# Kernel spectra from the compressed kernel in one dense matmul step; input spectra and tap sums in smaller TensorE tiles; a new task order

## The chip, the cores and the metric

The kernel runs on one core of a Trainium2 chip. The core has five engines that run their own instruction queues and wait for each other through semaphores: TensorE (PE, matmuls; its weight loads are listed apart as PEld), VectorE (DVE), ScalarE (ACT), GpSimd (POOL) and SyncE (SP, which issues transfers). Matmuls write to PSUM; DVE and ACT carry the results from there to SBUF (an "eviction"). Transfers between device memory and SBUF run on 16 DMA engines and are issued from the SP, POOL or ACT queue. The metric is the time of one execution on the device in microseconds (us); a profile is one execution recorded by the hardware profiler.

## What is computed

Two branches over the same input x (2048 positions, 640 channels, bf16), mixed by a gate. Branch A is attention with 32 heads of 20 channels in which each position sees eight positions at distances 0, 2, ... 14. Branch B is a state-space convolution: per channel a kernel K of length 2048, a real part of a sum over 192 complex exponentials, is convolved with the channel through a Fourier transform of length 4096.

```python
g = sigmoid((x * gate_w).sum(-1, keepdims=True))
# A
logits = einsum("bhsd,bhswd->bhsw", q, kg) * scale        # w: 8 taps, dilation 2
o = einsum("bhsw,bhswd->bhsd", softmax(logits), vg);  a = o @ wo
# B
l = arange(L).astype(bfloat16)                            # positions rounded to bf16
P = exp(logdA[:, :, None] * l)
K = einsum("dn,dnl,dn->dl", Cc, P, dB).real
y = irfft(rfft(u, 2 * L) * rfft(K, 2 * L))[:L] + u * Dskip
return g * a + (1 - g) * y
```

Since the positions are rounded to bf16, K takes few distinct values at large l: for each channel 32 x 20 values (times 8 i + m with i below 32 and m from a list of 20, `MS`, plus one more m, 2048, for the last four positions, 21 in all) hold the whole kernel. This is the "compressed kernel", tile E.

## The kernel before

Every piece of work is a task with an engine, an estimated duration and dependencies. Two plans exist, "main" and "tail"; in each the order of the tasks is a list written into the source (`ORDER`, L52), which also says on which engine ("A" for ACT, "D" for DVE) an eviction runs. `Plan.emit` (L150) issues them in that order, and each engine and each transfer queue works strictly in order.

Main plan. (1) SSM parameters (`SSMParams`, DVE and ACT, the first 40 us). (2) The input is turned and projected to q, k, v (`plan_late`, matmul L311, PSUM tile "tb"); v goes to device memory (vS). (3) The kernel generator (`KGen.plan`): ten chunks of 16 channels a group, each with 15 argument matmuls (L801, PSUM "ar"), 15 sine or exponential activations on ACT (L816, L818) into a ring of buffers, products on DVE (L838, L840: "pt", "qq") and 256 small matmuls (L856, PSUM "kps"), evicted to E. After five chunks a half of the channels ("hf") is complete. (4) Attention (`plan_core`) in eight tiles of 256 positions: for each the shifted v is fetched (`loadv`, "vc", L368, POOL queue), products on DVE ("prod", L375), logits on PE (L381), a softmax, the weights written to memory and fetched spread over the partitions ("asb", L428), products with v on DVE ("pv", L449), the sum over the taps on PE (`gather`, L456), and the output projection (L480) whose result is scaled by the gate ("ga", L489) and stored (gaS). Before, the partitions of "vc" are 64 rows of heads and halves times two groups of taps, each group holding four taps in its free dimension, and `gather` runs as 128x64 tiles of the PE array, two of them side by side.

(5) Kernel expansion (`KExpand`, L875): for each half, E is shifted between partitions by two small matmul groups (L895), copied out on DVE into the full kernel in time order (X, 11 copies, L903), written to memory (Kx, L929 to L932) and read back transposed (kc, L938). (6) First Fourier step (`first`, L1300, and `split`, L1319): matmuls of 256 columns with the constants F1k for the kernel and F1c for the input (Usb), evicted 1024 elements a partition to bufA (kernel) and big (input). The input's first step has to wait for the last generator product, since the ring lies in big.

Tail plan (`fft_conv`, L1024). For each of eight frequency blocks, the second Fourier step: four spectra (kernel and input, real and imaginary part) in two halves each, four matmuls of 320 columns per half (L1073, PSUM "fp") with a basis PHI, evicted as "sp_k" and "sp_u"; then six products and sums on DVE ("ta", "tc" L1101, "Y" L1104). Then the inverse transform in two steps (L1134, evictions "bufA<-cp"; L1164) and the mix with the gate, the attention result (gaF) and the store (L1170 to L1191). Transfers for the tail's constants (psi) and gaF are paced by the blocks (L1087).

Of the kernel before, what the change touches and what calls it, by code (L numbers as in the profile page):

```python
# [11 lines left out]
ALU = mybir.AluOpType  # L12
# [8 lines left out]
S = 2048  # L21
D = 640
# [5 lines left out]
VW = 256 + 3 * DIL  # L28
# [10 lines left out]
def _attn_consts():  # L39
    ind = np.zeros((128, 96), np.float32)  # L40
    for h in range(32):
        ind[4 * h:4 * h + 4, h] = 1.0
    for r in range(64):
        ind[[r, 64 + r], 32 + r] = 1.0
# [49 lines left out]
), "tail": (  # L94
# [21 lines left out]
class Plan:  # L116
# [21 lines left out]
    def order(self):  # L138
        out, at = [], 0
        for x in ORDER[self.name].split():  # L140
            at += int(x.rstrip("ADSG"))
            t = self.tasks[at]
            t.eng = x[-1] if x[-1] in "ADSG" else next(iter(t.dur))
            out.append(t)
        for n, t in enumerate(out):
            t.place = n
        assert len(out) == len(self.tasks) and all(d.place < t.place for t in out for d in t.deps + t.after)
        return out
# [20 lines left out]
class Attn:  # L169
# [80 lines left out]
    def consts(self, cst):  # L250
        nc = self.nc
        ind_np, ident_np, mask0_np = _attn_consts()
        self.ind = cst.tile([128, 96], BF16, name="ind")
# [7 lines left out]
    def load_wo(self, _):  # L261
        wv = self.wo.rearrange("(r a e) c -> a r e c", a=2, e=5)
        for a in range(2):
            self.nc.gpsimd.dma_start(self.wo_sb[64 * a:64 * a + 64], wv[a])
# [1134 lines left out]
```

## Time and profile before

| | |
|---|---|
| time, median of three runs | 337.42 us (335.88 to 338.04) |
| span of the profiled execution | 335.4 us |
| busy: PE, weight loads | 285.5 us (85%), 171.0 us (51%) |
| busy: DVE, ACT, POOL | 294.2 us (88%), 293.4 us (87%), 62.3 us (19%) |
| transfers | 45.68 MB, mean 136 GB/s |
| granted TensorE clock, mean | 0.98 of full speed |

The span runs from the first to the last instruction; the time of a run also holds what lies around it. "Busy" for PE counts pipelined matmuls from start to modelled end, so that a busy PE is not one at its peak. In the views below a row of the groups reads: line, engine, operation, tile written <- tiles read, shapes, number of instructions | busy us together, mean ns of one | idle time of the engine just before them and what ended it. A row of the timeline begins with the start and the length in us. A row of the windows gives, for a stretch of time, the busy us (and the instructions) of PE, weight loads, DVE, ACT and POOL, the granted clock, the share of the DMA engines and GB/s.

### The profile page before, as it was taken

The page shows a single profiled execution, that of the slowest core. Times are in us where ns is not written, and L with a number is a line of the kernel's source. Part 1 is how long each engine was busy: PE and PEld are TensorE (multiplying, and loading weights), DVE is VectorE, ACT ScalarE, POOL GpSimd, SP SyncE. Part 2 cuts the span into 40 slices and gives each one's busy share as a digit, 9 for nine tenths or more (in the row PEclk, how much of TensorE's full clock was granted, in tenths as well). Part 3 has the DMA queues.
Part 4 walks back from the last instruction along what each step waited for, and adds up shares of the span by engine and source line. Part 5 has one row for each costly group of instructions (what it writes and reads, how often), then busy time and mean ns, then how long its engine had stood idle before and what let it go on. Part 6 is the DMA issues. An engine that isn't in the chain of part 4 may idle for free. (4 is left out here: it accounts for less than half of the span.)

```text
span 335.4 us, 11982 instructions
## 1 busy us (share of the span) xinstructions
PE 285.5 (85%) x5181; PEld 171.0 (51%) x5214; DVE 294.2 (88%) x401; ACT 293.4 (87%) x433; POOL 62.3 (19%) x94
## 2 busy tenths in 40 slices
PE   0367999997899999999998799999999899996850
PEld 0334563444445555445554344556677676665740
DVE  1997988798989999999999979999686799999881
ACT  1789736999899999999999799999987889998990
POOL 8700043020005000101412341211040000000062
PEclk9999999999999999999999989999999999999985
DMA  8984435437107110524874887365565527666056
GB/s 253 356 264 113 119 91 159 86 91 170 26 9 153 27 24 8 149 62 141 199 190 119 186 208 161 93 118 124 154 207 221 180 64 216 159 123 100 4 136 182
DMA packets 45975, 45.68 MB, mean 136 GB/s; under 512 B 25098, under 2 KB 39738, under 8 KB 45922
## 3 DMA queue, kind: packets, MB, share of 16 engines
q1 hardware_dynamic: 39928, 27.90, 30.3%
q0 software_dynamic: 5248, 16.39, 20.2%
q8 instruction: 41, 0.67, 0.9%
q10 hardware_dynamic: 746, 0.61, 0.6%
q14 instruction: 12, 0.10, 0.1%
HBM read 30.88 MB, written 14.01 MB: 134 GB/s over the span
## 5 line engine op out<-in xcount | busy, mean ns | idle before, releaser
L311 PE MATMUL tb<-bufA 128*128 128x512 bf16 x267 | 73.5, 391 | 4.2 <-issue 1.4
L816 ACT ACTIVATE big<-ar 128x740 bf16<-128x740 int16 (+1 forms) x72 | 56.7, 858 | 1.4 <-PE ar L801 1.2
L818 ACT ACTIVATE big<-ar 128x848 bf16<-128x848 f32 x60 | 50.1, 905 | 0.2
L801 PE MATMUL ar<-Rarg,L 64*128 64x212 bf16 (+4 forms) x600 | 46.5, 253 | 3.5 <-ACT big L816 1.9
L449 DVE TENSOR_TENSOR pv<-vc,asb 128x2048 bf16<-128x2048 bf16 x40 | 48.2, 1217 | 0.3 <-PE tb L456 0.3
L311 PEld LDWEIGHTS <-bufA 128*128 128x128 bf16 x300 | 31.2, 122 | 28.5 <-issue 12.3
L856 PEld LDWEIGHTS <-pt 128*32 128x32 bf16 (+1 forms) x2560 | 25.3, 92 | 35.7 <-issue 33.2
L856 PE MATMUL kps<-qq,pt 128*32 128x21 bf16 (+1 forms) x2560 | 36.6, 173 | 6.0 <-issue 5.1
L838 DVE TENSOR_TENSOR pt<-big 128x1024 bf16<-128x1024 bf16 x48 | 32.8, 701 | 4.3 <-ACT big L816 2.2
L801 PEld LDWEIGHTS <-L 64*128 64x128 bf16 x600 | 20.8, 94 | 25.2 <-issue 22.4
L480 PE MATMUL tb<-wo_sb,oT 128*128 128x320 bf16 x160 | 29.9, 306 | 0.2
L507 ACT ACTIVATE sp_u<-fp 128x640 bf16<-128x640 f32 x31 | 23.9, 953 | 0.8 <-PE fp L1073 0.8
L375 DVE TENSOR_TENSOR prod<-prj 128x2048 bf16<-128x2048 bf16 x20 | 24.0, 1218 | 0.2 <-PE lg L381 0.2
L375 DVE TENSOR_TENSOR prod<-qA,kA 128x2048 bf16<-128x2048 bf16 x20 | 23.9, 1217 | 0.2 <-PE lg L381 0.2
L507 ACT ACTIVATE sp_k<-fp 128x640 bf16<-128x640 f32 x29 | 22.6, 969 | 1.1 <-PE fp L1073 1.1
L456 PE MATMUL tb<-pv,ind 128*64 128x512 bf16 (+1 forms) x192 | 23.2, 353 | 0.0
L368 POOL DMA_DIRECT2D vc<-vS x16 | 11.5, 723 | 59.0 <-DVE pv L449 55.0
L840 DVE TENSOR_TENSOR qq<-big 128x1344 bf16<-128x1344 bf16 x24 | 21.2, 883 | 0.0
L1191 POOL DMA_DIRECT2D out_dram<-ot x14 | 7.7, 558 | 72.3 <-DVE ot L1173 72.3
L1073 PEld LDWEIGHTS <-PHI 128*128 128x128 bf16 x160 | 15.5, 97 | 8.1 <-issue 1.1
L489 ACT ACTIVATE ga<-tb,g_sb 128x320 bf16<-128x320 f32 x29 | 15.6, 550 | 3.4 <-PE tb L480 3.1
L480 PEld LDWEIGHTS <-oT 128*128 128x128 bf16 x160 | 13.1, 98 | 7.1 <-issue 3.1
(171 smaller groups left out, 547.9 us busy)
## 6 DMA issues: line engine op xcount, KB each, us to landing
vc<-vS POOLq DMA_DIRECT2D x16, 327.5 KB, 6.4
xn<-in_A_x_dram SPq DMA_DIRECT2D x4, 640.0 KB
gaS<-ga SPq DMA_DIRECT2D x8, 320.0 KB
Usb<-in_A_x_dram POOLq DMA_DIRECT2D x8, 320.0 KB, 5.7
gaF<-gaS SPq DMA_DIRECT2D x8, 320.0 KB
bufA<-in_A_wqkv_dram SPq DMA_DIRECT2D x3, 800.0 KB
Sprm<-pc SPq DMA_DIRECT2D x10, 240.0 KB
L<-Sprm SPq DMA_DIRECT2D x76, 30.0 KB
```

The lines of the kernel that those rows point to most:

```text
L311: nc.tensor.matmul(ppf, self.wq[:, which, kt, e::5], self.xT[:, c0 // 1024, kt, c0 % 1024:c0 % 1024 + SC], start=(kt == 0), stop=(kt == NK ...
L375: nc.vector.tensor_tensor(b[e][:], q[:, e, o:o + C].unsqueeze(1).to_broadcast([128, W, C]), win(k[:, e, :], o, W, DIL, C), ALU.mult)
L449: nc.vector.tensor_tensor(o, vw, b["asb"][:].unsqueeze(2).to_broadcast(sh), ALU.mult)
L456: nc.tensor.matmul(b["op", e][64 * a:64 * a + 64, 0:n, :], ind[:, 32:96], b["pv", e][:, w, a, 0:n, :], start=(w == 0), stop=(w == 3), skip ...
L480: nc.tensor.matmul(apf[:, :320], b["oT"][:, e, i * 128:(i + 1) * 128], wo_sb[:, e, hf * 320:(hf + 1) * 320], start=(e == 0), stop=(e == 4))
L507: nc.scalar.activation(o, i, ACT.Identity)
L801: nc.tensor.matmul(ar[:, g2, a0:a0 + ncol], L[rows, sb, gv, l0:l0 + 128], R[rows, c0:c0 + ncol], start=True, stop=True, tile_position=(64 ...
L816: nc.scalar.activation(d_[:, :, s0 * QW:s1 * QW], ar[:].bitcast(I16)[:, :, 0:2 * (s1 - s0) * QW:2], ACT.Sin, scale=SCL)
L818: nc.scalar.activation(dst[:, gp::2].rearrange("p g s n -> p g (s n)"), ar[:, :, 0:2 * EW], ACT.Exp)
L838: nc.vector.tensor_tensor(pt[:, :, k, :], gg[:, :, ::-1] if k else gg, e1, ALU.mult)
L840: nc.vector.tensor_tensor(qq[:], trg[:, :, KI:].rearrange("p a (v m) -> p a v m", v=2), exq[:, :, KI:].unsqueeze(2).to_broadcast([128, 32, ...
L856: nc.tensor.matmul(kps[32 * g:32 * g + 32, h, NM * ql:NM * ql + NM], pt[rows, k, v, :], qq[rows, k, v, :], start=(g not in started), stop= ...
```

## The change

1. The expansion of the kernel and its first Fourier step are dropped. A constant "km" of 128 x 20,480 values (eight blocks of 640 KB) maps the 640 compressed values of a channel directly to its 2048 frequencies: contraction over 128 partitions (32 i times four m) and five steps k. The class KSpread stores E of a half to memory with four transfers and reads it back with m on the partitions (tile T); `dense` does 20 matmuls of 160 columns for two of a block's four f. They run on 128x64 tiles of the array, two side by side, with km as the weights and T as the moving data.
2. Half 0's kernel spectra for all eight blocks are made in the main plan (`spectra`, 16 evictions of 640 elements), half 1's in the tail, block by block ("kd", 16 evictions). The blocks of the tail run in the order 5, 6, 7, 0, ... 4, since the last three km tiles of the main plan stay in their three slots.
3. The input's Fourier steps use 64x64 tiles of the array: `first` does 16 matmuls of 128 columns where it did four of 256, and the second step ("up") 16 matmuls of 160 columns for a half spectrum where it did four of 320.
4. Attention's shifted v is laid out as 32 heads times four groups of two taps: four copies a tile of 256 positions (32 rows, all groups) instead of two; "asb" is one transfer of half the bytes; `gather` runs on 128x32 tiles, four side by side, with half the columns per PE pass, and in smaller tasks; wo is laid out to match (four loads).
5. The term of the kernel's last four positions (m = 2048) is no longer in the kernel spectrum: POOL works out running sums of the first input rows times that value (`lag`), and eight small matmul pairs ("sel") add it in the last step.
6. A new order of all tasks, with other choices between ACT and DVE: E evictions 10 and 0 become 7 and 3, "ga" 29 and 3 become 22 and 10, v evictions 7 and 3 become 4 and 6.

```diff
-class KExpand:
...
+class KSpread:
...
+    def store(self, hf, E):
+        for mm in range(4):
+            self.nc.sync.dma_start(self.Ed[hf, mm].rearrange("g i c k -> (g i) c k"), E[:, :, 5 * mm:5 * mm + 5].rearrange("p c m x -> p c (m x)"))
+    def load(self, hf):
+        for mm in range(4):
+            self.nc.sync.dma_start(self.T[hf][32 * mm:32 * mm + 32].rearrange("i g c k x -> i g (c k x)"), self.Ed[hf, mm].rearrange("g i c k -> i g (c k)"))
+def dense(nc, o, km, T, ro, fs):
+    for f in fs:
+        for k in range(5):
+            for h in range(2):
+                rhs = bass.AP(T.tensor, T[:, 0, 0, k, 20 * h].offset, [list(T.ap[0]), [400, 4], [220 - 40 * h, 2], [1, 20]])
+                nc.tensor.matmul(o[64 * h:64 * h + 64, f, 0:160].rearrange("p (g j x) -> p g j x", j=2, g=4), km[:, k, ro, f, :], rhs,
+                                 start=(k == 0), stop=(k == 4), skip_group_check=True, tile_position=(0, 64 * h))
+def dense_out(nc, en, dst, o):
+    evict(nc, en, dst.rearrange("p j (x g) f -> p (j x) g f", g=4), o[:, :, 0:160].rearrange("p f (g x) -> p x g f", g=4))
...
+    def load_km(n, fb):
+        o = KM0 + KMW * (n % 3)
+        nc.sync.dma_start(P["bufA"][:, o:o + KMW], km_d[:, fb])
...
-                b["vc"] = aq.tile([128, 2, 5, VW], BF16, name="vc")
-                for w2 in range(2):
-                    nc.gpsimd.dma_start(b["vc"][64 * w2:64 * w2 + 64]...)
+                b["vc"] = aq.tile([128, 4, 5, VW], BF16, name="vc")
+                for w4 in range(4):
+                    nc.gpsimd.dma_start(b["vc"][32 * w4:32 * w4 + 32]...)
...
+                    for t in range(2):
+                        for a in range(4):
+                            nc.tensor.matmul(b["op", e - e % 2][32 * a:32 * a + 32, e % 2, :], ind[:, 32:64], b["pv", e][:, t, a, :], start=(t == 0), stop=(t == 1),
+                                             skip_group_check=True, tile_position=(0, 32 * a))
...
+            for j in range(2):
+                for hh in range(2):
+                    nc.tensor.matmul(up[64 * hh:64 * hh + 64, j, 160 * fl:160 * fl + 160], ph[64 * j:64 * j + 64, 4 * (fb % 2) + f, kind, :],
+                                     Bu()[64 * j:64 * j + 64, 2 * (4 * fb + f) + ri, j ^ hh, :], start=(ri == 0), stop=(ri == 1), skip_group_check=True, tile_position=(64 * j, 64 * hh))
...
+        def lag(_):
+            U = P["Usb"][:, 0:4]
+            cu = now["kk"].tile([128, 4, 160], F32, name="cu", tag="xkc")
+            nc.gpsimd.tensor_copy(cu[:, 0], U[:, 0])
+            for s in range(1, 4):
+                nc.gpsimd.tensor_tensor(cu[:, s], cu[:, s - 1], U[:, s], ALU.add)
+            for hf in range(2):
+                for g in range(4):
+                    nc.gpsimd.tensor_tensor(P["W"][r]..., cu[r]..., half[hf][r, :, 20, :]..., ALU.mult)
```

On the queues the new transfers stand like this. SP: after the loads of the generator's eighth chunk E of half 0 is stored and read back and the first km tile is loaded; the other km loads stand between the last two chunks' "L" loads, the softmax weights and the stores gaS; E of half 1 is stored after the last "asb" and read back behind the gaS store of the last tile but one. POOL: basis tile 2 is loaded at the start, tiles 3 and 0 behind `lag`, which stands behind the last "vc" fetch; tile 1 comes on SP in the tail.

More of the change, by code (lines that the diff above doesn't have):

```diff
@@ L146, in order @@
             t.place = n
-        assert len(out) == len(self.tasks) and all(d.place < t.place for t in out for d in t.deps + t.after)
+        own = set(map(id, out))
+        assert len(out) == len(own) == len(self.tasks) and all(d.place < t.place for t in out for d in t.deps + t.after if id(d) in own)
         return out
@@ L522 @@
 NM = len(MS)
-FIRST = 13
 SW = 4 * (KI + 2 * NM)
@@ L1046, in fft_conv @@
     ends, muls, turned, paces, last = [], {}, [], [], None
[L1047 to L1063 removed]
+    kms = list(P["kms"])
@@ new lines, in fft_conv, with late_consts @@
+    sel = sb.tile([128, 64], BF16, name="sel")
+    def late_consts(_):
+        P["load_phi"](1, nc.sync, sb)
+        nc.sync.dma_start(sel[:], P["sel_d"])
+    P["phl"][1] = pl.add("phi1", "S", 0.6, late_consts, dma=1.7)
+    for n in range(8, 13):
+        kms.append(pl.add(f"km{n}", "S", 0.4, lambda _, n=n: P["load_km"](n, FB[n - 5]), after=kms[-1:], acq=["km"], dma=2.6))
+    for s, fb in enumerate(FB):
+        spec, sp = {}, {}
+        nk = 5 + s
+        ks = bufA[:, KS0 + 1280 * (s % 2):KS0 + 1280 * (s % 2) + 1280].rearrange("p (r j x f) -> p r j x f", r=2, j=2, f=4)
+        for ro in range(2):
@@ L1091, in paced @@
+        def paced(_, s=s):
+            if s < 4:
+                nc.sync.dma_start(psi[:, 16 * s:16 * s + 16], psi_d[:, 16 * s:16 * s + 16])
+            for k in ((), (), (), (0,), (1, 2), (3, 4), (5, 6, 7), ())[s]:
                 j, h = k // 2, 16 * (k % 2)
                 nc.sync.dma_start(gaF[32 * j:32 * j + 32, h:h + 16], gr[j // 2, j % 2][:, h:h + 16])
-        if fb < 7:
-            paces.append(pl.add(f"paced{fb}", "S", (0.4, 0.4, 0.4, 0.8, 0.8, 0.8, 1.2)[fb], paced, deps=es, after=paces[-1:] or early, dma=(2.1, 2.1, 2.1, 3.4, 2.7, 2.7, 4.0)[fb]))
+        if s < 7:
+            paces.append(pl.add(f"paced{s}", "S", (0.4, 0.4, 0.4, 0.8, 0.8, 0.8, 1.2)[s], paced, deps=es, after=paces[-1:], dma=(2.1, 2.1, 2.1, 3.4, 2.7, 2.7, 4.0)[s]))
@@ L1116, in fft_conv @@
                 ps.append(p1)
             for ro in range(2):
-                last = pl.add(f"Y{fb}{k}{ro}", "D", w, lambda _, f=add, x=(x0, x1), ro=ro: f(_, x[0], x[1], ro), deps=[heads[ro], ps[ro]], after=[last])
-                for cb in range(x0 // 4, x1 // 4):
-                    muls[cb, ro] = last
+                last = pl.add(f"Y{fb}{k}{ro}", "D", w, lambda _, f=add, hs=hs, ro=ro: f(_, hs, ro), deps=[heads[ro], ps[ro]], after=[last])
+                for h in hs:
+                    for cb in range(10 * h, 10 * h + 10):
+                        muls[cb, ro] = last
@@ L1257, in gated_mix_kernel, with spread @@
         xdone = late + [gate[0]]
-        half = {}
-        def expand(hf, f):
-            shift, move, near, own, other, store = kx.expand(hf, lambda: half["E"], now, pa, kg.S12)
-            a = pl.add(f"shift{hf}", "D", 0.13, shift, deps=[f, dsk])
-            n1 = pl.add(f"move{hf}", "P", 0.72, move, deps=[f], acq=["ar"], eq=1120)
-            if hf == 0:
-                kg.moved = n1
-            n2 = pl.add(f"near{hf}", "AD", {"A": 0.57, "D": 0.72}, near, deps=[n1], rel=[("ar", n1)])
-            o1 = pl.add(f"own{hf}", "D", 2.2, own, deps=[a], after=[at.stored[1, 2], at.stored[2, 2]])
-            half["own"] = o1
-            o2 = half["cp"] = pl.add(f"other{hf}", "D", 1.0, other, deps=[o1, n2])
-            st = [pl.add(f"xst{hf}{e}", e, d, store, deps=[o2], dma=w) for e, d, w in (("S", 1.25, 4.0), ("G", 0.6, 1.6))]
-            def fetch(e, hf=hf):
-                if (hf, "kc") not in half:
-                    half[hf, "kc"] = now["kk"].tile([128, 64, CH], BF16, name="kc", tag="xkc")
-                kx.load(hf, half[hf, "kc"], int(e == "G"), nc.sync if e == "S" else nc.gpsimd)
-            half[hf, "ld"] = [pl.add(f"xld{hf}{e}", e, d, fetch, deps=st, dma=2.6) for e, d in (("S", 0.5), ("G", 0.6))]
+        half, tld = {}, {}
+        def spread(hf, f):
+            E = lambda: half[hf][:]
+            a = pl.add(f"skip{hf}", "D", 0.13, lambda _: kx.skip(hf, E()), deps=[f, dsk])
+            st = pl.add(f"est{hf}", "S", 1.4, lambda _: kx.store(hf, E()), deps=[a], dma=1.8)
+            tld[hf] = pl.add(f"tld{hf}", "S", 1.4, lambda _: kx.load(hf), deps=[st], dma=1.8)
         def fin(c, b, m, m0, fins):
@@ L1282, in fn @@
                 if cl == 0:
-                    half["E"] = now["kk"].tile([128, NM, CH], BF16, name="E")
-                evict(nc, en, half["E"][:].rearrange("p m (c x) -> p c m x", c=2)[:, :, :, CQ * cl:CQ * cl + CQ],
-                                      b["kps"][:, :, 0:CQ * NM].rearrange("p c (q m) -> p c m q", m=NM))
-            f = pl.add(f"fin{c}", "AD", {"A": 0.4, "D": 0.47}, fn, deps=[m] + ([half["cp"]] if c == HC else []), after=fins[-1:], rel=[("kb", m0)])
+                    half[hf] = now["kk"].tile([128, 2, NM, CQ * HC], BF16, name=f"E{hf}")
@@ L1287, in fin @@
+                evict(nc, en, half[hf][:, :, :, CQ * cl:CQ * cl + CQ], b["kps"][:, :, 0:CQ * NM].rearrange("p c (q m) -> p c m q", m=NM))
+            f = pl.add(f"fin{c}", "AD", {"A": 0.4, "D": 0.47}, fn, deps=[m], after=fins[-1:], rel=[("kb", m0)])
             if cl == HC - 1:
-                expand(hf, f)
+                spread(hf, f)
             return f
-        kg.plan(pl, pa, pk, late[:30] + xdone[-1:], params, opened, fin)
-        def first(name, src, dst, n, deps, after):
+        fins = kg.plan(pl, pa, pk, late[:30] + xdone[-1:], params, opened, fin)
@@ L1293, in first @@
+        def first(n, deps, after):
             b = {}
             def mm(_):
-                sf = src()[:].rearrange("p a b -> p (a b)")
-                st = sf.shape[1] // 128
+                st = P["Usb"]
                 b["bp"] = pa.tile([128, 4, 256], F32, name="bp", tag="ar")
                 for ql in range(4):
-                    nc.tensor.matmul(b["bp"][:, ql, :], sf[:, 4 * n + ql::st], P["F1c" if name == "fu" else "F1k"][:], start=True, stop=True)
-            def ev(en):
-                d_ = now["big"][:].rearrange("p (c f q g) -> p c f q g", c=NCH, f=64, q=8) if dst is None else dst
-                evict(nc, en, d_[:, n // 2, :, 4 * (n % 2):4 * (n % 2) + 4, :].rearrange("p f q g -> p f (q g)"),
-                      b["bp"][:].rearrange("p q (g f) -> p f (q g)", f=64))
@@ new lines, in ev, with spectra, kd @@
+            def ev(en):
+                x = 4 * n
+                o = 80 * (x // 40) + 4 * (x % 20)
+                evict(nc, en, Bu()[:, :, x % 40 // 20, o:o + 16].rearrange("p f (q g) -> p f q g", q=4), b["bp"][:].rearrange("p g (q f) -> p f q g", f=64))
+            m = pl.add(f"fu{n}", "P", 0.24, mm, deps=deps, after=after, acq=["ar"], eq=1024)
+            P["fue"].append(pl.add(f"fue{n}", "AD", {"A": 0.905, "D": 1.13}, ev, deps=[m], rel=[("ar", m)]))
+        def spectra(n, kms):
+            K0 = P["bufA"][:, 1280 * n:1280 * n + 1280].rearrange("p (r j x f) -> p r j x f", r=2, j=2, f=4)
+            prev = []
+            for ro in range(2):
+                b = {}
+                def kd(_, h, ro=ro, b=b):
+                    if h == 0:
+                        b["kd"] = pa.tile([128, 4, 256], F32, name="kd", tag="ar")
+                    dense(nc, b["kd"], P["KM"][n], P["T"][0][:], ro, (2 * h, 2 * h + 1))
+                m = pl.add(f"kd0{n}{ro}0", "P", 0.68, lambda _, f=kd: f(_, 0), deps=[tld[0], kms[n]], after=prev, acq=["ar"])
+                m2 = pl.add(f"kd0{n}{ro}1", "P", 0.68, lambda _, f=kd: f(_, 1), deps=[m], rel=[("km", kms[n])] if ro else [])
+                prev = [m2]
+                P["kde"].append(pl.add(f"ke0{n}{ro}", "AD", {"A": 0.59, "D": 0.735}, lambda en, ro=ro, b=b: dense_out(nc, en, K0[:, ro], b["kd"]), deps=[m2], rel=[("ar", m)]))
```

365 lines of the change are left out of this document (159 added, 206 removed), and 90 rows, old and new, of the table ORDER.

## The prediction

> **What bounds the kernel now.** I read the span and clock first, then busy time by stage, then the order of time around the stage borders, and last the groups of instructions. The chain of waits says little here: it covers only the last 13 us (output scaling, "ACT tt L1170"), which the change leaves as it is.
>
> ```profile
> core 0: 335.4 us, clock 0.980
> ...
> core 0: us, PE busy (x) PEld busy (x) DVE busy (x) ACT busy (x) POOL busy (x), PEclk, DMA share, GB/s
> 60.00:225.00 165.00, 153.92 (x3502) 80.71 (x3527) 153.48 (x207) 159.84 (x237) 29.18 (x42) 0.99 0.47 111
> 0.00:232.30 232.30, 201.44 (x4042) 108.25 (x4076) 209.16 (x277) 206.80 (x296) 50.27 (x72) 0.99 0.51 131
> 225.30:267.40 42.10, 39.67 (x522) 29.17 (x522) 34.47 (x49) 37.10 (x53) 5.82 (x10) 1.00 0.55 177
> 232.30:270.30 38.00, 35.77 (x335) 26.77 (x336) 29.07 (x42) 32.17 (x49) 4.37 (x8) 1.00 0.57 183
> 266.60:305.40 38.80, 36.34 (x258) 24.80 (x260) 36.49 (x52) 36.12 (x60) 0.00 (x0) 1.00 0.60 143
> 0.00:266.50 266.50, 233.54 (x4349) 132.35 (x4382) 236.66 (x315) 236.87 (x339) 54.64 (x80) 0.99 0.52 140
> ```
>
> The borders of these windows come from the timeline: the last sine/exponential of the kernel generator on ACT, the last generator product on DVE, the first spectrum matmul, the first spectrum product, the first inverse matmul.
>
> ```profile
> 223.84 1.46 ACT L816 ACTIVATE bufA<-ar 128x740 bf16<-128x740 int16 x2
> 231.39 0.89 DVE L840 TENSOR_TENSOR qq<-bufA,big 128x1344 bf16<-128x1344 bf16 x1
> 266.64 0.70 PE L1073 MATMUL fp<-bufA,PHI 128*128 128x320 bf16 x4 [0.91 <-ACT bufA L507]
> 270.29 1.56 DVE L1101 TENSOR_TENSOR ta<-sp_u,sp_k 128x1280 bf16<-128x1280 bf16 x2 [0.21 <-ACT sp_u L507]
> 305.38 2.42 PE L1134 MATMUL cp<-GAB,Y 64*128 64x128 bf16 x80 [2.42 <-DVE Y L1104]
> ```
>
> From 60 to 225 us ACT is 97% busy, PE and DVE 93%: ACT paces that stretch. Between the generator's end and the first product ("hand-over", 232.3 to 270.3) DVE is busy 29.1 of 38.0 us, because kernel values go to memory and back and then through evictions. In the spectrum stage PE and DVE are both full (36.3 and 36.5 of 38.8), so work has to leave both there.
>
> **Vector work: evictions and copies.** The kernel's first transform step and its expansion go.
>
> ```profile
> L507 ACT ACTIVATE bufA<-bp 128x1024 bf16<-128x1024 f32 x13 | 13.1, 1036 | 1.0 <-PE bp L1300 1.0
> L509 DVE CAST bufA<-bp 128x1024 bf16<-128x1024 f32 x2 | 2.4, 1219 | 0.1
> L507 ACT ACTIVATE bufA<-tb 128x512 bf16<-128x512 f32 x6 | 3.3, 607 | 0.0
> L509 DVE CAST bufA<-tb 128x512 bf16<-128x512 f32 x4 | 2.6, 685 | 0.1
> L903 DVE COPY X<-E 128x80 bf16<-128x80 bf16 (+5 forms) x16 | 3.3, 282 | 0.5 <-PE bp L1300 0.5
> L903 DVE COPY X<-nxt 128x80 bf16<-128x80 bf16 (+2 forms) x6 | 1.4, 298 | 0.0
> L507 ACT ACTIVATE sp_k<-fp 128x640 bf16<-128x640 f32 x29 | 22.6, 969 | 1.1 <-PE fp L1073 1.1
> L491 DVE TENSOR_SCALAR ga<-tb,g_sb 128x320 bf16<-128x320 f32 x3 | 1.6, 546 | 1.0 <-ACT big L507 1.0
> ```
>
> Removed: 16.4 us on ACT (13.1 + 3.3), 9.7 on DVE (2.4 + 2.6 + 3.3 + 1.4). The 32 kernel-spectrum evictions stay, again 640 elements each (0.78 us, 22.6/29), but 16 of them, 12.5 us, move from the spectrum stage to the main part. The new order spends the relief on balance: DVE takes seven more "ga" scalings (7 x 0.546 = 3.8 us) and some projection evictions from ACT. Going through the emitted order with these durations, ACT's list up to its last sine is as long as before (13 dense evictions in, as much out), and DVE's list up to its last generator product is about 4 us longer (three ga, three v and three E evictions against the X copies of one half). So the generator does not end earlier: ACT at 225, DVE at 232.3 + 4 = 236, less some of the 23.1 us that DVE idles before 232.3. I take 2 us off: 234.
>
> **The hand-over.** After its last product DVE's list holds ten tap multiplications, four casts of input spectra, six ga, two evictions and small things.
>
> ```profile
> L449 DVE TENSOR_TENSOR pv<-vc,asb 128x2048 bf16<-128x2048 bf16 x40 | 48.2, 1217 | 0.3 <-PE tb L456 0.3
> L509 DVE CAST big<-bp 128x1024 bf16<-128x1024 f32 x5 | 6.1, 1221 | 2.7 <-PE bp L1300 2.7
> L507 ACT ACTIVATE big<-bp 128x1024 bf16<-128x1024 f32 x15 | 14.9, 1036 | 0.5 <-PE bp L1300 0.4
> kc<-Kx POOLq DMA_DIRECT2D x2, 640.0 KB, 5.0
> 249.61 0.34 SPq L938 DMA_DIRECT2D kc<-Kx  x1
> 79.16 9.35 SPq L766 DMA_DIRECT2D L<-Sprm  x8
> L368 POOL DMA_DIRECT2D vc<-vS x16 | 11.5, 723 | 59.0 <-DVE pv L449 55.0
> vc<-vS POOLq DMA_DIRECT2D x16, 327.5 KB, 6.4
> L1003 POOL COPY pace<-Usb 32x2 bf16<-32x2 bf16 x7 | 6.1, 865 | 22.6 <-DMA Usb<-in_A_x_dram 22.5
> ```
>
> That is 10 x 1.22 + 4 x 1.22 + 6 x 0.55 + about 1.8 = 22 us up to the spectra, with 2.5 us of idle 24.5: first spectrum matmul at 258.5, against 266.6. ACT has 16 x 0.99 + 6 x 0.54 + about 8 = 27 us after 225.3 (37.1 before), so 252 to 256: DVE is what is late. The compressed kernel values (E, 410 KB a half, eight SP issues at about 0.4 us) must be back by then: E is complete at about 244 (9.6 us into DVE's list); two transfers, each at most the 5.0 us of the kc load plus 1.6 us of issue, end at 257. Covered by some 2 us; each microsecond beyond that is a microsecond of the end. The v tiles are now cut in four copies: 32 issues of 0.72 us on POOL instead of 16, and twice the bytes. The last one starts when the taps of the last tile but two are done, about 3.5 us before 234, issues 2.9 us and lands 6.4 us later, near 240; its taps stand 11 us after 234. Covered by 5 us. Two loads of the Fourier basis stand on POOL behind the new work there ("lag", 12 operations; the nearest row, the pace copies, has 0.87 us each). Its last four wait for E: 244 + 3.5 + 1.1 of issue + 6 of landing is 255, and the second block, which needs them, comes at 263.
>
> **PE.** Columns first.
>
> ```profile
> 269.35 0.71 PE L1073 MATMUL fp<-bufA,PHI 128*128 128x320 bf16 x4
> 269.90 1.79 PE L1073 MATMUL fp<-big,PHI 128*128 128x320 bf16 x12
> 152.24 1.06 PE L456 MATMUL tb<-pv,ind 128*64 128x512 bf16 x12
> 312.68 3.45 PE L1134 MATMUL cp<-GAB,Y 64*128 64x128 bf16 x112 [0.28 <-ACT bufA L507]
> 317.42 2.59 PE L1164 MATMUL yp<-bufA,psi 64*64 64x160 bf16 x128 [1.29 <-DVE bufA L509]
> L456 PEld LDWEIGHTS <-ind 128*64 128x64 bf16 x192 | 8.4, 109 | 6.4 <-issue 3.4
> ```
>
> Eight more matmuls of 320 columns cost 1.79 - 0.71 = 1.08 us: 0.42 ns a column. Two 64-column tiles do run at once: the twelve of L456 (eight of 512, four of 256 columns) would take 5120 x 0.42 / 2 = 1.08 us and took 1.06. With short matmuls and a weight load each it is 15 to 20% over: L1134 30.8 ns against 26.9, L1164 20.2 against 16.8.
>
> Main part: out go 80 matmuls x 256 columns (8.6 us); the input step and the tap sums in four tiles at once halve (8.6 to 4.3, 17.2 to 8.6 us); in come 640 dense matmuls x 160 x 0.42 / 2 = 21.5 us. The sum is zero. The changes of tile shape on PE fall from 359 to 282 in the emitted order; the main part's columns make 168 us and PE is busy 233.5, so a change costs about 0.18 us, and 77 fewer are 14 us of PE that it gets back; none of it is on ACT's path, so I count only the 2 us above.
>
> Spectrum stage, per block of eight: 64 input matmuls at 20.2 ns = 1.29 us, 80 dense ones, three shape changes 0.54. For a dense one the bounds are 33.6 ns (streams fill it, as in L456) and 78 (its load, 8.4/192 = 44 ns, in the open). I take 37, a tenth over the stream, between L456 and L1134: 2.96 us. Together 4.8 us, 38.3 for eight; before 256 x 0.135 = 34.6.
>
> ```profile
> L1104 DVE TENSOR_TENSOR Y<-ta,tc 128x1280 bf16<-128x1280 bf16 (+2 forms) x20 | 12.9, 682 | 0.0
> L1101 DVE TENSOR_TENSOR tc<-sp_u,sp_k 128x1280 bf16<-128x1280 bf16 (+2 forms) x20 | 12.9, 682 | 0.0
> L1101 DVE TENSOR_TENSOR ta<-sp_u,sp_k 128x1280 bf16<-128x1280 bf16 x16 | 12.5, 818 | 0.4 <-ACT sp_u L507 0.2
> ```
>
> DVE's products stay: 12.9 + 12.9 + 12.5 = 38.3 us. Their kernel operand now jumps between two halves; pv, whose operand is cut finer, runs at 0.59 ns an element against 0.64 here, so I count nothing. Gone are two of four evictions on DVE (1.6 us); the last block is cut in halves instead of a fifth and two rests, which starts the inverse about 0.8 us later. So the stage takes about what it took, 38.7 us from first spectrum matmul to first inverse, plus 0.8: 258.5 + 39.5 = 298. From there to the end nothing changes but eight tiny matmul pairs: 335.4 - 305.4 = 30.0. Span 328. The median of the runs shown, 337.42, is 2.0 above the profiled span, so **330 us**.
>
> [...]
>
> **Rivals.**
> 1. *Weight loads in the open, slower.* At 78 ns a block takes 6.2 + 1.29 + 0.54 = 8.1 us on PE, 64 for eight, 26 more than DVE needs: about 355 us. It decides from 37 ns on (then PE passes DVE) and has eaten the whole gain at 37 + 7.4/0.64 = 49 ns. L456 and L1164, 64 columns wide at 20 ns a pair, speak against it. 0.13.
> 2. *The round trip of E is late*, since SP is in order and the loads of T stand behind a store that waits for ga. Five us too late: 335. The 2 us of cover are thin; 0.12.
> 3. *The main part is held up by transfers.* Taps of twice the bytes and eight basis loads of 640 KB add some 7 MB to the 18 MB of 60:225 (DMA share 0.47, so about 0.65), and the fourth basis load waits on SP for a slot with eight "L" loads behind it. A generator 7 us late gives 337. For it: eight L issues already take up to 9 us; against: no wait for L shows in that stretch. 0.08.
> 4. *More than I count.* The 14 us of PE in the main part shorten DVE's idle by 9 more: 321. 0.12.
>
> That the change does not do what it says can be left out: the emitted order shows the removed instructions gone.
>
> **Numbers.** Forecast 0.55 (325 to 334). Range 320 to 340: it leaves out rival 1 and the better half of rival 4. This kernel's runs spread by 0.6%, so about 1% can be told from no change. Faster by over 1% (under 334.0): 0.55 + 0.12 = 0.67; within: 0.20 (rivals 2, 3); slower: 0.13.
>
> **What would show it.** Groups "kd" near 0.75 us for 20 matmuls in a row confirm the price of the dense step; 1.0 or more is rival 1, with DVE idle before "ta". PE waiting for T before its first tail "kd" is rival 2; "L" or "asb" issued late, with ACT idle before 225, rival 3. First spectrum matmul at 258 and 39 us from there to the first inverse confirm the sum. Wrong if the last sine moves by more than 4 us either way.

## The result and the profile after

| | before | changed |
|---|---|---|
| time, median of four runs | 336.96 us (335.88 to 338.04) | 386.85 us (383.75 to 388.07) |
| span of the profiled execution | 335.4 us | 385.3 us |
| last generator sine (ACT), last product (DVE) | 225.3, 232.3 | 263.9, 269.8 |
| first spectrum matmul, first inverse matmul | 266.6, 305.4 | 300.8, 353.8 |
| granted TensorE clock, mean | 0.98 | 0.91 |

The changed kernel takes 1.148 times as long, 95% interval 1.141 to 1.155. In all tables the median is of all executions of a kernel, the ratio leaves out those over 1.5% above its fastest, and the profiles of e6, e7, e9 and e13 below are of such slower ones. Against the forecast span of 328 us it loses 57 us: 42 before the first spectrum matmul (300.8 against 258.5), 13.5 in the spectrum stage (53.0 against 39.5), 1.5 behind it. Busy times on the page of after:

```profile
PE 305.4 (79%) x7015; PEld 201.4 (52%) x7038; DVE 294.0 (76%) x380; ACT 279.1 (72%) x399; POOL 79.4 (21%) x119
```

ACT has 14 us less to do and DVE as much as before. PE is busy 20 us longer (285.5 before), but 45 of its busy us fall into stretches of half clock; in e9 and e13 below, which keep every matmul and have 11 and 14 us of half clock, it is busy 295 and 294 us, so at most some 9 us are more work. What is to be explained in the main is idle time and the lower clock. The windows of after, cut at the stage borders of the table:

```profile
140.00:180.00 40.00, 36.97 (x861) 21.14 (x866) 37.88 (x52) 37.44 (x56) 4.34 (x6) 1.00 0.45 114
180.00:210.00 30.00, 20.04 (x622) 13.61 (x616) 17.42 (x22) 16.36 (x24) 6.95 (x12) 0.77 0.92 189
210.00:240.00 30.00, 24.09 (x512) 14.76 (x512) 19.53 (x26) 20.85 (x31) 5.99 (x11) 0.89 0.75 168
240.00:269.80 29.80, 26.00 (x741) 19.48 (x742) 21.79 (x28) 19.89 (x30) 6.95 (x11) 0.89 0.60 134
269.80:300.80 31.00, 26.42 (x636) 18.71 (x634) 23.59 (x23) 21.19 (x28) 13.57 (x15) 0.89 0.48 121
300.80:353.80 53.00, 40.92 (x1152) 37.17 (x1153) 36.44 (x51) 29.60 (x46) 0.00 (x0) 0.87 0.68 164
```

From 140 to 180 us ACT is still nearly full, and the generator is hardly late: the 19th of its 30 products on DVE ("qq") ends at 176.5 us, 5 us later than before, the last one 37 us later. From 180 to 210 no engine is full: PE 20 of 30 us, DVE 17, ACT 16, with the DMA engines at 0.92 and the granted clock at 0.77. What PE waits for in the two kernels, from the views of waits (total us, times, longest), before first:

```profile
PE kps L856 <- issue: 5.1, 4, 2.4
```

```profile
PE kps L832 <- issue: 17.1, 6, 5.3
PE kd L875 <- issue: 11.3, 7, 3.6
PE tb L443 <- issue: 5.4, 2, 4.6
PE tb L304 <- DVE prj L496: 5.2, 1, 5.2
```

"Issue" means that no semaphore explains the wait. The timeline shows where such a wait falls:

```profile
188.86 0.95 PE L832 MATMUL kps<-qq,pt 64*32 64x21 bf16 x96
189.74 0.49 PE L777 MATMUL ar<-Rarg,L 64*128 64x74 bf16 x4
190.16 0.61 PE L443 MATMUL tb<-pv,ind 128*32 128x256 bf16 x5
195.37 0.40 PE L443 MATMUL tb<-pv,ind 128*32 128x256 bf16 x3 [4.61 <-issue]
```

PE stops between the fifth and the sixth of eight matmuls that depend on nothing new. Counting along the emitted instructions of PE, weight loads included, that stop stands ahead of number 6072; the other long ones stand at 2746, 5816, 6840, 8120, 9652, 11442, 12462 and 12718, the three of before at 1468, 6074 and 6842. Divided by 256 they all leave a remainder between 174 and 188. Among the DMA queues the pages list one with packets of the kind "instruction" (count, MB, share), before first:

```profile
q8 instruction: 41, 0.67, 0.9%
```

```profile
q8 instruction: 55, 0.90, 1.0%
```

The number of PE's instructions rose from 10,430 to 14,078, which is 40.7 and 55.0 times 256; with 1280 fewer the queue has 50 packets (e5 below), with 768 fewer 52 (e10). So in these kernels one packet, of 16 KB, stands for 256 instructions of PE, called a block of code here. The times of the packets can be set beside PE's progress. In the last row, where the DMA share is 0.33 from 256.6 to 275.2 us, the packet of the next block starts as PE enters a block; in the others it starts later:

```
PE enters  its 256 instr.  packet of the next    PE goes on
block at   are done at     block runs (us)       at
179.1      183.9           184.8 to 186.2        187.8
187.8      190.8           192.8 to 193.9        195.4
207.5      209.7           212.4 to 213.6        215.1
240.4      242.6           243.7 to 244.7        246.0
256.6      275.2           256.6 to 257.7        (no wait; kernel before)
```

In these rows a stop arises where PE is through its 256 instructions before the next block has come: after 2.2 to 4.8 us in the first four, while in the last one they take 18.6 us. The packet itself takes 1.0 to 1.4 us; ahead of it lie, in the first four rows, 3.3 to 5.7 us in which the DMA engines are full with other transfers (share 1.03 to 1.07 in the windows). From one border to the next PE then needs 5.6 to 8.7 us. Stops of 0.4 us and more at such borders, up to the inverse transform, add up to 4.9 us before and 33.6 us after.

The clock follows. The windows of after right behind two of the stops:

```profile
215.10:221.00 5.90, 5.90 (x119) 2.73 (x121) 3.38 (x5) 2.90 (x4) 0.41 (x2) 0.50 0.73 193
345.40:350.00 4.60, 4.55 (x70) 4.32 (x73) 0.82 (x1) 0.70 (x1) 0.00 (x0) 0.50 0.71 111
```

In all the record of the granted clock has 58 us at half speed between 30 us and the inverse transform, in nine stretches of 3.4, 6.8 or 13.7 us, before one of 3.4 us. A stop of 2.0 us (to 113.5) was followed by such a stretch, from 115.2 us, while one of 1.9 us before (to 84.3) was followed by none; what decides this was not shown.

### The profile page after: what moved, and what is told of

Read it like the earlier page. It is cut to its first block, busy times and chain, and to the rows that moved or that the text cites. A ratio compares the mean times of both kernels' runs of the same rounds, so it can differ in the third digit from the quotient of the medians.

```text
span 385.3 us, 15615 instructions
## 1 busy us (share of the span) xinstructions
PE 305.4 (79%) x7015; PEld 201.4 (52%) x7038; DVE 294.0 (76%) x380; ACT 279.1 (72%) x399; POOL 79.4 (21%) x119
## 5 line engine op out<-in xcount | busy, mean ns | idle before, releaser
L875 PE MATMUL kd<-T,bufA 128*64 128x160 bf16 x1280 | 58.3, 251 | 11.6 <-issue 11.3
L875 PEld LDWEIGHTS <-bufA 128*64 128x64 bf16 x1280 | 52.3, 119 | 16.6 <-issue 15.0
L777 PE MATMUL ar<-Rarg,L 64*128 64x212 bf16 (+4 forms) x600 | 49.3, 260 | 2.7 <-ACT big L794 0.9
L494 ACT ACTIVATE bufA<-kd 128x640 bf16<-128x640 f32 x31 | 21.8, 704 | 30.3 <-PE kd L875 29.7
L832 PE MATMUL kps<-qq,pt 128*32 128x21 bf16 (+1 forms) x2560 | 27.1, 176 | 17.3 <-issue 17.1
L361 POOL DMA_DIRECT2D vc<-vS x32 | 21.8, 688 | 73.4 <-DVE pv L436 69.5
L832 PEld LDWEIGHTS <-pt 128*32 128x32 bf16 (+1 forms) x2560 | 23.2, 93 | 25.3 <-issue 23.9
L1080 DVE TENSOR_TENSOR ta<-sp_u,bufA 128x1280 bf16<-128x1280 bf16 x16 | 13.0, 824 | 12.9 <-ACT bufA L494 12.9
L494 ACT ACTIVATE sp_u<-up 128x640 bf16<-128x640 f32 x30 | 19.3, 711 | 4.0 <-PE up L1029 4.0
L443 PE MATMUL tb<-pv,ind 128*32 128x256 bf16 x320 | 16.8, 296 | 5.8 <-issue 5.4
```

The costliest lines, as they stand in the source:

```text
L361: nc.gpsimd.dma_start(b["vc"][32 * w4:32 * w4 + 32].rearrange("h a e s -> h (a e) s"), sv[:, :, c0 + 2 * DIL * w4:c0 + 2 * DIL * w4 + VW])
L494: nc.scalar.activation(o, i, ACT.Identity)
L777: nc.tensor.matmul(ar[:, g2, a0:a0 + ncol], L[rows, sb, gv, l0:l0 + 128], R[rows, c0:c0 + ncol], start=True, stop=True, tile_position=(64 ...
L832: nc.tensor.matmul(kps[32 * BLOCK[g]:32 * BLOCK[g] + 32, h, NM * ql:NM * ql + NM], pt[rows, k, v, :], qq[rows, k, v, :], start=(g not in s ...
L875: nc.tensor.matmul(o[64 * h:64 * h + 64, f, 0:160].rearrange("p (g j x) -> p g j x", j=2, g=4), km[:, k, ro, f, :], rhs, start=(k == 0), s ...
```

## The experiments

A short table first. e1 and e8 leave out fetches of vc, e2 loads of km, e3, e9 and e13 both; e5 puts two dense matmuls into one; e7 does all of this. e15 is e9 with two dense matmuls in one in the main plan, e10 and e14 are e9 with less dense work there (e13 is e9 again, e14 is e10 again). e6 undoes part 4, e11 spreads the fetches of vc, and e4 and e12 change the kernel before. MB is what the DMA engines moved; stops are those at borders of code blocks, up to the inverse transform; the next three columns are the last generator product, the first spectrum matmul and the length of the spectrum stage in the profiled execution; the ratio is to the kernel before.

| kernel | MB | stops, us | product | spectrum | stage | time, us | ratio (95%) |
|---|---|---|---|---|---|---|---|
| before | 45.7 | 4.9 | 232.3 | 266.6 | 38.7 | 337.0 | 1 |
| changed | 53.2 | 33.6 | 269.8 | 300.8 | 53.0 | 386.9 | 1.148 (1.141-1.155) |
| e1 | 45.3 | 17.6 | 255.6 | 284.5 | 49.9 | 365.9 | 1.083 (1.061-1.105) |
| e2 | 46.7 | 23.4 | 262.4 | 293.7 | 43.5 | 372.5 | 1.102 (1.079-1.125) |
| e3 | 38.8 | 13.9 | 251.3 | 278.6 | 43.7 | 356.2 | 1.054 (1.034-1.074) |
| e4 | 51.0 | 1.8 | 241.1 | 276.9 | 38.7 | 347.1 | 1.027 (1.009-1.046) |
| e5 | 53.2 | 27.8 | 274.9 | 305.4 | 40.2 | 379.0 | 1.122 (1.112-1.131) |
| e6 | 49.1 | 15.9 | 252.7 | 281.8 | 49.7 | 363.9 | 1.068 (1.056-1.080) |
| e7 | 37.4 | 10.2 | 247.9 | 277.7 | 39.5 | 344.5, 350.3 | - |
| e8 | 44.0 | 15.3 | 245.7 | 272.9 | 49.9 | 355.2 | 1.051 (1.042-1.060) |
| e9 | 37.4 | 12.2 | 246.0 | 273.5 | 42.2 | 341.0, 348.3 | - |
| e10 | 37.4 | 10.2 | 237.3 | 264.7 | 43.9 | 341.4 | 1.014 (1.007-1.021) |
| e13 | 37.4 | 14.3 | 244.3 | 273.1 | 43.1 | 348.2 | 1.024 (1.016-1.033) |
| e14 | 37.4 | 10.7 | 237.0 | 264.2 | 44.0 | 341.9 | 1.016 (1.011-1.021) |
| e15 | 37.4 | 12.0 | 242.1 | 270.3 | 42.8 | 345.9 | 1.031 (1.026-1.037) |
| e11 | 53.3 | 17.4 | 272.2 | 317.8 | 48.2 | 400.9 | 1.191 (1.183-1.199) |
| e12 | 45.7 | 1.4 | 238.7 | 273.6 | 38.7 | 344.9 | 1.025 (1.020-1.030) |

**Transfers taken away (e1, e2, e3) or added to the kernel before (e4).**

```diff
 e1    def loadv(_, c0=c0, b=b, sc=sc):
+          if sc > 1:
+              b["vc"] = self.vcs[sc % 2]; return
 e2    def load_km(n, fb):
+          if n < 3:
               nc.sync.dma_start(P["bufA"][:, o:o + KMW], km_d[:, fb])
 e4 (before)
-          for w2 in range(2):
+          for w2 in (0, 1, 0, 1):
```

> The changed kernel, but the shifted v (vc) is fetched for the first two attention tiles only; the other six tiles work on those old values, so 24 of 32 transfers (7.7 MB) are left out, and the attention output is not the reference's. Instructions on PE, DVE and ACT are the same. Theory A (TensorE's instructions come in blocks of 256 over the same DMA engines; the bigger transfers hold the blocks up, and TensorE stands still at the block borders): the stops of 1 us and more within a matmul group between 100 and 250 us fall from about 20 us to under 8, and the time falls by 15 to 25 us, to 362-372. Theory B (more TensorE instructions, whatever is transferred, make the code late): stops and time stay, 380-388. Theory C (dense matmuls with their weight loads in the open): 380-388, stops stay.

> The changed kernel, but only the first three of the 13 loads of the dense constant km (640 KB each) are made; the ten others, 6.6 MB, are left out, and the later frequency blocks use old values, so the convolution's output is not the reference's. Theory A: the stops at block borders near 185-195 us and in the tail (313 to 346 us) go, and the time falls by 12 to 22 us, to 365-375. Theories B and C: 380-388, the stops in the tail stay.

> Both omissions together (14.3 MB less than the changed kernel, 39 MB in all, less than the 45.7 of the kernel before). Theory A: hardly any stop at a block border is left (under 8 us in all), the clock stays near 0.98, and the time is 335-350. Theories B and C: above 375.

> The kernel before, but every fetch of vc is issued twice (5.2 MB more, 16 more issues on the POOL queue, the result unchanged; not one TensorE instruction more). Theory A: the start of TensorE's code blocks is delayed by more than 3 us about ten times instead of five, stops at block borders grow from about 6 us to 12 or more, and the time rises by 4 to 12 us. Theory B (only the number of instructions counts): within 1% of 337.

Not one instruction of PE fewer, and the time falls by 21, 14 and 31 us: theory B and C fall as sole causes. But e3, with less traffic than the kernel before, keeps 13.9 us of stops and 356 us, above the range given, and e2 keeps its stops near 190 us, where the first three km loads stand, and half of those in the tail (4.5 of 8.8 us). And e4 was right in its time for a wrong reason: its stops fell to 1.8 us, and the time came from one wait of 10.6 us of a "pv" on DVE, with PE behind it, when POOL's queue issued vc fetches late. So traffic alone does not make the stops either: before, with 51 MB, has hardly any.

**The number of instructions, and part 4 undone (e5, e6).** In e5 the dense matmuls take 320 columns, half as many of them:

```diff
-    for f in fs:
+    for f in fs[:1]:
         for k in range(5):
             for h in range(2):
-                rhs = bass.AP(..., [[400, 4], [220 - 40 * h, 2], [1, 20]])
-                nc.tensor.matmul(o[64 * h:64 * h + 64, f, 0:160]..., km[:, k, ro, f, :], rhs, ...)
+                rhs = bass.AP(..., [[800, 2], [200, 4], [1, 40]])
+                nc.tensor.matmul(o[64 * h:64 * h + 64, f:f + 2, 0:160]..., km[:, k, ro, f + h, :], rhs, ...)
```

> The changed kernel with every two dense matmuls of 160 columns put into one of 320 columns (same weights tile shape, same number of columns through PE, same transfers; 640 matmuls and 640 weight loads fewer, five of 55 code blocks). The kernel spectra are not the reference's. Theory A alone (transfers set how late code is, the number of instructions does not matter): stops at block borders stay above 30 us (33.5 in the changed kernel), 381-388. Theory D (a stop comes where 256 instructions run faster than a block's fetch takes, so density and transfers multiply): the stops inside dense groups (11 us) go, the others stay, 20 to 25 us in all; time 366-375.

> Part 4 of the change undone: the shifted v again as 64 rows times two groups of four taps (two copies a tile, 5 MB less), asb in two transfers, the tap sums on 128x64 tiles, 8 matmuls of 256 columns for each of five e, so the same number of TensorE instructions; the rest is the changed kernel with its order. Theories A and D: stops fall from 33.5 to 20 to 26 us, time 366-375 in spite of some 8 us more PE work. If only the number of instructions counted: 385-395.

e5 splits the case in two; over the whole kernel its stops (27.8 us) and its time (379.0) lie between what theories A and D gave. In the spectrum stage theory D holds: the stage shrinks from 53.0 to 40.2 us with every transfer in place, and one stop of 0.8 us is left in it. In the main part it does not help (305.4 against 300.8): there the stops lie mostly in runs of "kps" matmuls, which were not changed, and the borders only moved to other places.

```profile
PE kps L832 <- issue: 20.7, 8, 5.3
```

In the tail of the changed kernel each frequency block has 64 input and 80 dense matmuls, with their loads 288 instructions in the 4.9 us that were forecast for it: 256 in 4.4 us, where before 64 instructions filled the same time. That is less than the 5.6 to 8.7 us that PE needed from border to border under traffic.

e6, the attention part as before, gave 363.9 us with half the vc bytes: 23 us less, more than expected, although the tap sums stand in 128x64 tiles again, in which they kept PE busy for 23.2 us before (16.8 in the changed kernel).

**The softmax weights behind vc (e8), and everything light (e7).** e8 is e1 with `sc > 0`; e7 is e8, e2 and e5 together.

> As e1, but vc is fetched for the first tile only (the other seven work on old values): the second tile's fetch, 1.29 MB, no longer stands before the first softmax weights (asb) on the DMA engines. Theory E (asb, issued at 69.5 us, waits for that fetch, and DVE's first pv waits for asb 6.3 us with PE and ACT behind it): the stop of PE near 75 to 82 us goes (under 1.5 us), time 355-362. Rival (the order puts the first pv too early whatever is transferred): the stop stays at 5 us or more, time 363-369.

> vc fetched for the first tile only, km loaded three times only, and the dense step in matmuls of 320 columns: less transfer and fewer instructions together; neither branch's result is the reference's. Theory D: stops under 6 us, clock above 0.97, first spectrum matmul at 262-268 us, time 338-346. If it stays above 350, something else in the new order holds the main part up.

The stop of PE from 75 to 80 us is no code stop: PE waits there for DVE, and DVE for asb. The rows of after, SP's issue and DVE's wait, and the DMA queues from 66 to 75 us (packets, MB, share of the 16 engines):

```profile
69.45 0.60 SPq L420 DMA_DIRECT2D asb<-aS  x1
```

```profile
77.45 2.36 DVE L436 TENSOR_TENSOR pv<-vc,asb 128x2048 bf16<-128x2048 bf16 x2 [6.30 <-DMA asb<-aS]
```

```profile
q0 software_dynamic: 534, 1.92, 95.7%
q1 hardware_dynamic: 323, 0.06, 4.6%
```

POOL's queue (q0, the second tile's vc, then v) has nearly all of the engines, and SP's 128 KB land 8 us after their issue. Without that fetch the stop is gone (e8: 10.7 us less than e1), and with the smaller one of e6 the same instruction waits 0.3 us:

```profile
71.59 2.36 DVE L438 TENSOR_TENSOR pv<-vc,asb 128x2048 bf16<-128x2048 bf16 x2 [0.27 <-DMA asb<-aS]
```

e7 reaches the stage that was forecast (39.5 us), but its main part still ends at 247.9, not at 234, its stops are 10.2 us and its first spectrum matmul comes at 277.7, both above the ranges given; of its two times 344.5 lies in the range and 350.3 above it. Something else was left there.

**PE's own work in the main part (e9, e10, e13 to e15).** e9 is e8 and e2 together; e10 sums half 0's dense step over two of five steps. Their two times each did not settle it (341.0 and 348.3 against 341.1 and 341.7), so both were run again, with e15: e9 with the main plan's dense step as in e5.

```diff
 e10, e14 (main plan only)
-        for k in range(5):
+        for k in (0, 4):
```

> The changed kernel with vc fetched for the first tile only and km loaded three times only (15 MB less), all instructions kept; neither branch's result is the reference's. It is the base for the next run. Theory D: stops at block borders under 12 us, last generator product at 241-246 us, spectrum stage 43-45 us, time 343-350.

> As e9, but the dense step of half 0 in the main plan sums over two of its five steps (384 of 640 matmuls left out there; the evictions and the tail's dense step stay). Theory F (the dense step stands in 170 to 250 us, where PE is busy 27 of 30 us and ACT and DVE wait for it, while the tap sums and the old first step leave PE earlier: PE paces the end of the main part): the last generator product comes 6 to 11 us earlier than in e9, and the time falls by as much. Rival (ACT's list sets the generator's end, as predicted): under 3 us earlier.

> The kernel of e9 once more (vc for the first tile only, km three times), timed often, since its two times lay 7 us apart (341.0 and 348.3) and the gap to e10 in the profiles (6.6 us of span) was not clear in the times. Base for the next two. Expected 342-347.

> The kernel of e10 once more (as e13, with the main plan's dense step over two of its five steps). Theory F (PE's work paces the end of the main part): 5 to 9 us below e13, 335-341. If the gap in the profiles was chance: within 3 us of e13.

> As e13, but the main plan's dense step in 320 matmuls of 320 columns instead of 640 of 160: the same columns through PE, half the instructions; half 0's spectra are not the reference's, the tail's dense step stays. If it is PE's work that paces (theory F): within 3 us of e13. If it is the number of instructions (code blocks): as far below e13 as e14 is, 335-341.

The windows from 180 to 240 us of e13, then of e14, then of e15:

```profile
180.00:210.00 30.00, 27.74 (x763) 18.83 (x764) 22.86 (x30) 21.92 (x32) 9.94 (x13) 0.88 0.39 88
210.00:240.00 30.00, 27.92 (x780) 19.58 (x779) 29.04 (x32) 25.34 (x38) 11.36 (x12) 1.00 0.18 45
```

```profile
180.00:210.00 30.00, 26.32 (x641) 14.99 (x645) 27.04 (x35) 26.22 (x40) 9.21 (x15) 0.94 0.41 92
210.00:240.00 30.00, 23.81 (x665) 15.89 (x658) 29.74 (x34) 23.80 (x36) 10.97 (x10) 1.00 0.19 48
```

```profile
180.00:210.00 30.00, 26.10 (x631) 16.43 (x633) 23.97 (x32) 23.23 (x34) 8.15 (x10) 1.00 0.43 96
210.00:240.00 30.00, 28.01 (x662) 17.54 (x659) 27.15 (x32) 24.86 (x38) 12.28 (x14) 0.94 0.17 45
```

With the whole dense step PE is busy 26 to 28 of the first 30 us, DVE and ACT 22 to 24; without 60% of it DVE and ACT come to 26 to 27. The first spectrum matmul moves from 273.1 to 264.2, in e9 and e10 from 273.5 to 264.7. In the times e13 spreads widely (342.4 to 349.3), and its interval overlaps e14's; but e15 and e14, which have 52 code blocks each and differ in PE's work, lie apart: 1.031 (1.026 to 1.037) against 1.016 (1.011 to 1.021), some 5 us, and in their profiles the first spectrum matmul stands at 270.3 and 264.2, 6.1 us apart. e15, with half of these instructions, shows no gain over e13 that is clear of the noise. So theory F holds, at 5 to 6 us; the 8.8 us of the other two pairs are its upper end.

**The same bytes, spread (e11, e12).** Before each vc copy but a tile's first, POOL reads two elements of the copy before, and so waits until that has landed (5.0 and 5.4 us in two such rows of e12):

```diff
+                    if w4:
+                        r = slice(32 * w4 - 32, 32 * w4)
+                        nc.gpsimd.tensor_copy(self.vpace[r], b["vc"][r, 0, 0, 0:2])
                     nc.gpsimd.dma_start(b["vc"][32 * w4:32 * w4 + 32]...)
```

> The changed kernel with its four copies of a vc tile issued one after another: before each copy but the first, POOL copies two elements of the copy before it, and so waits for its landing. Same bytes, same TensorE instructions, 24 small POOL copies more; at most 322 KB of vc under way instead of 1.29 MB. If what holds the code blocks up is the queue that a whole tile's fetch makes: stops fall from 33.5 to 20 us or less, PE's wait at 75 to 82 us goes, time 360-374. If the bytes alone count: stops stay near 33 us, 380-390. If the taps come late instead (four landings of about 4 us each): DVE waits for vc, 385 or more.

> The kernel before with the same pacing of its two vc copies a tile (327 KB each). Its three stops at block borders (1.9, 2.4, 0.6 us) and the half clock after one of them are worth some 6 us at most; if the vc fetch makes them, the time falls by 1 to 4 us, ratio 0.988 to 0.998; if other transfers make them, ratio 0.998 to 1.004; if POOL's queue comes late by the waits, as in e4, 1.005 or more.

The stops halve at equal bytes (33.6 to 17.4 us), so the bytes alone do not set them. How much of this is the shorter queue is not shown: the taps come late instead, PE waits 28.9 us for "pv", which may have given later blocks time to arrive, and the stops at 5816 and 6072 are still 2.6 and 4.2 us long. The kernel is the slowest of all. DVE's waits in e11:

```profile
DVE pv L440 <- DMA vc<-vS: 29.1, 4, 11.0
```

In e12 the three stops shrink to one of 1.4 us, and 8 us are lost on POOL's queue, as in e4.

No kernel tried beats the one before; of the changed ones that leave nothing out, e6 is the fastest.

## Why the prediction was wrong

It said faster, 330 us. It is wrong in sign, and outside its range.

- *The main part, "ACT at 225, DVE at 234".* Failed, by 39 and 36 us. The sum went through ACT's and DVE's lists with durations and took PE's code to be there. The failing step is the one on PE: "77 fewer are 14 us of PE that it gets back; none of it is on ACT's path". PE came onto everybody's path by stops at its code blocks (22.1 us up to 270 us, and half clock behind them), and once these are reduced, by its own work (e14, e15). Nor did it get 14 us back, and the 0.18 us for a change of tile shape behind that figure was an estimate that no run shows by itself: up to the first spectrum matmul it is busy 233.5 us before, 246.3 in the changed kernel, and in e9, with 11 us of half clock, still 241.9.
- *Rival 3, "held up by transfers", 337 us, 0.08.* The right place and the wrong mechanism and price. Transfers were looked for where they are waited for by name ("L", "asb", km). asb was late by one such wait of 6.3 us. The large part is a wait that no row names but "issue": taking 15.8 MB away (e9, e13) brings the first spectrum matmul from 300.8 to 273. The trace of before had the row: four waits of "kps" for "issue", 5.1 us, one of them right among the transfers near 190 us. The prediction did not read it.
- *The hand-over, 24.5 us.* It took 31.0 (269.8 to 300.8), with 2.6 us of stops and half clock from 279.0 to 285.9. In e9 and e14 it is still 27.5 and 27.2 us; where these 3 us come from is open.
- *"The sum is zero" for PE's columns in the main part.* Not even over the whole part, since the input step, which was to halve, did not: eight old matmuls and the 32 that replace them take the same 1.1 us (below, before, then e9), some 4 us in all. And where it matters it was far from zero: the tap sums' relief is spread over 160 us, and the dense step falls into the last 80.

```profile
248.14 1.04 PE L1300 MATMUL bp<-F1c,Usb 128*128 128x256 bf16 x8
```

```profile
268.79 1.11 PE L1290 MATMUL bp<-F1c,Usb 64*64 64x128 bf16 x32
```

- *Dense matmul at 37 ns, rival 1 at 78 ns.* The price was right. Row of e3 at full clock, and of e5 with twice the columns:

```profile
298.72 1.59 PE L880 MATMUL kd<-T,bufA 128*64 128x160 bf16 x40
```

```profile
337.83 2.91 PE L875 MATMUL kd<-T,bufA 128*64 128x320 bf16 x40 [0.35 <-ACT bufA L494]
```

  1.59/40 = 40 ns with the pipeline's end in it, 2.91/80 = 36 ns for 160 columns, where the prediction estimated 33.6 for the columns alone and 44 for a load: in these two rows the weight loads are nearly hidden. The group mean of after (58.3 us for 1280 matmuls, 45.5 ns) is that price with half clock in it, not rival 1.
- *The stage, 39.5 us.* Right where hardly any stops are left, which only the runs with half the dense instructions reach (e5 40.2, e7 39.5), wrong as it stands (53.0): 8.8 us of stops and 13.6 us at half clock. Taking away the five km loads of the tail gives 43.5 (e2), and halving the dense instructions gives 40.2.
- *Rival 2, E's round trip.* Did not come: the view of waits has no wait of PE for T.
- *The rest, 30.0 us.* 31.5.

Laid end to end: of the 42 us before the first spectrum matmul, 27 go with 15.8 MB of vc and km (6 of them the wait for asb), 6 to 9 with 60% of the main dense step, and the 6 to 9 left are about e14's own stops there (6.9). What share is the stops themselves and what the half clock behind them was not separated: no run keeps the clock up through the long stops. An estimate bounds it: PE was busy for 45 us at half clock, and at full speed this takes no less than half as long, so half clock cost it at most some 23 us. Nor was the new order of tasks tried alone; it sets how densely the "kps" runs follow each other, and may have a part in the main stops.

## What to carry to other kernels

Before trading few long matmuls for many short ones, count the instructions and the time that 256 of them take, stage by stage, and compare that with what a block of code needs there (5.6 to 8.7 us in the four rows under traffic); the trace of before had the sign here, a row of PE waiting 5.1 us for "issue". Transfers whose consumer was covered held up code here (33.6 us of stops, 12.2 and 14.3 in e9 and e13 with 15.8 MB less) and another queue (asb landed 8 us after its issue while POOL's queue had 95.7% of the engines): price extra bytes by the stretch in which the DMA engines are full, not by whether their consumer is covered. And add up an engine's work in the stretch where a step will stand, not over the whole part.

## What the hardware showed that was not expected

- In the five rows of packets the next block's packet starts 0 to 5.7 us after PE has entered the block ahead of it, never earlier, and one that started 5.0 us after that (at 192.8) was missed at the very next border: PE was through at 190.8 and went on at 195.4. Up to the inverse transform PE stood still at such borders for 33.6 us.
- POOL's two-element copies, 0.2 us at best, took 7 to 10 us at times in e4 and e12, with the vc fetches queued behind them; why was not settled. From e12:

```profile
204.10 10.45 POOL L1007 COPY pace<-Usb 32x2 bf16<-32x2 bf16 x1 [4.31 <-DMA Usb<-in_A_x_dram]
215.29 0.72 POOL L372 DMA_DIRECT2D vc<-vS  x1
```
